# Two routings of a mixture-of-experts kernel: gate fills and ScalarE's order in the first, the layout of the list and the place of small steps in the second

## The chip, the core and the metric

The kernel runs on one core of one Trainium2 chip. A core has five engines, each with its own queue of instructions that it works through in order: TensorE (PE in the profile, its weight loads PEld), VectorE (DVE), ScalarE (ACT), GpSimd (POOL) and SyncE (SP), which here only starts DMAs. The metric is device time in microseconds (us). The kernel before takes 647.91 us, the median of three runs of 646.74 to 649.23.

## The reference

```python
X = np.fft.fft(x, axis=1); X = np.fft.fft(X, axis=2)      # x: 8 x 3072 x 256
x = X.real.reshape(24576, 256)
# first mixture: 8 experts, 256 -> 1024 -> 256
P = exp(x @ w_gate - max)
for _ in range(8):                                         # rows, then columns
    P /= P.sum(1) + 1e-9;  P /= P.sum(0) + 1e-9;  P *= N / E
x = sum over e of P[:, e] * (relu(x @ w1[e]) @ w2[e])
# second mixture: each row to the one expert with the largest logit
e = argmax(x @ w_gate2);  g = softmax(x @ w_gate2)[e]
out[row] = g * (relu(x[row] @ u1[e]) @ u2[e])
```

The logits are so spread that nearly all weights of the first mixture are zero in float32. The kernel computes the few (row, expert) pairs that count, and checks that there are not more than it has room for; otherwise a dense version would run.

## The kernel before, in words

There are five stages. The Fourier stage (lines 23 to 279) makes the transformed rows, writes them to the DRAM tensor H and keeps the 194 x 8 logits of each partition in SBUF. The first routing (`route1`) finds the pairs that count, gives each a slot in one of 29 tiles of 128 rows (three per expert and five free ones), and writes the row number of each slot into the list `Rhidx`. GpSimd then gathers the rows from H, and the first experts run. The second routing (`route2`) assigns the 29 tiles' rows to the second experts and makes the list `Rgidx` of 30 tiles; the rows are gathered from the DRAM tensor acc, and the second experts run, which scatter to the output. Each expert is a first product (line 914, eight blocks of 1024 hidden columns), relu into a high and a low part (lines 900 on ScalarE and 901 through the helper line 438 on VectorE), and a second product (line 947), with each float32 operand split into two parts.

A list is made by matmuls. VectorE makes for each slot column a 0/1 table `ah` of the row within a tile (`irx` compared with `rb`, 24, 24 and 16 columns at a time in the first routing, 10, 10 and 9 in the second) and a 0/1 table `oh` of the tile (`itx` compared with `tb`). From `oh` come two values, both in the tile `bv`: one by VectorE (times the entry `ja` or `t1`), one by ScalarE (times the partition number). TensorE multiplies `ah` of a column with both values of it, one matmul for each column, all added up in one PSUM tile `pl` (line 569 in the first routing, where values lie in runs of four columns, line 562 in the second, where a tile's columns lie 29 apart). VectorE reads the sums and writes the list.

While VectorE works on the first routing, TensorE has filler work: sixteen gate fills (`gates2`, line 1277), each 8 float32 matmuls that prepare the second gate's columns `g2` from the tables `w2t` of the eight experts, two fills for each, evicted from PSUM by ScalarE (line 1279) into two PSUM buffers in turn. The tables of experts 0 to 2 and 6 lie in the buffers rawa, rawb, rawc, and rawc again; those of 3, 4, 5 and 7 in `w1h`/`w1l` and `w2h`/`w2l`. The second fill of an expert below 4 issues the next load on SP's queue. The string table `G2` says where the fills stand: entry k is issued by `fill(k)` at the k-th hook of `route1` ("g" is a fill, "0" to "3" a piece of the first expert's weights whose high part ScalarE makes and whose low part is kept for VectorE later, "l" writes the logits to DRAM, "z" zeroes parts of the output and of acc, "v" is two warm-up matmuls with zeros).

At the end of a routing the rows of the first expert's three tiles come by gathers of 128 rows each (line 816), are turned by six transposes (line 867, `moe.turn`), and taken from PSUM by ScalarE as `xh` (line 870) and VectorE as `xl`; then line 914 begins. Warm-up matmuls (line 1296, `warm(n)`: n matmuls of 512 columns with zeros) stand before and after the list of the second routing (W3 and W4 of them) and between the transposes (three after each pair). `Slots` hooks small steps between the blocks of an expert: slot (0, i) comes after block i of the first product of expert 0.

Of the kernel before, what the change touches and what calls it, by code (L numbers as in the profile page):

```python
# [9 lines left out]
BF16 = mybir.dt.bfloat16  # L10
I32 = mybir.dt.int32
AF = mybir.ActivationFunctionType
ALU = mybir.AluOpType
# [350 lines left out]
NSL = 40  # L364
NS2 = 8
NSA = NSL + 3 * NS2
# [80 lines left out]
class Route:  # L447
# [5 lines left out]
    def C(self, n):  # L453
        a, w = self.K["off"][n]
        return self.K["cst"][:, a:a + w]

    def positions(self, T, M, n, rst, nf_, hook=lambda: None, S=None, n1=None):

# [15 lines left out]
        if two:  # L474
# [14 lines left out]
        nc.vector.tensor_tensor_scan(pos.rearrange("p e s -> p (e s)"), rst, m2.rearrange("p e s -> p (e s)"),  # L489
                                     0.0, ALU.mult, ALU.add)  # L490
        o.ts(oi, oi, 7, ALU.logical_shift_right)
# [38 lines left out]

    def split(self, T, gp, cs, n, nm):

        o = self.o
        a, g = T([n], name="ga" + nm), T([n], name="gs" + nm)
        tb, rb = T([n], BF16, name="tb" + nm), T([n], BF16, name="rb" + nm)
# [9 lines left out]
        return tb, rb, gp  # L545

# [25 lines left out]
def route1(nc, rt, L, rmx, K, R, keep, pool, ring, hooks):  # L572
# [88 lines left out]
    def spans(g0, g1, by):  # L661
        g = slice(g0, g1)
        wide = lambda v: v.rearrange("p (g s) -> p g s", s=RUN)[:, g, None, :].to_broadcast([128, g1 - g0, NT1, RUN])
        o.tt(oh[:, g], K["itx"][:, g], wide(tb), ALU.is_equal)
        o.tt(bv[:, g, 0], oh[:, g], wide(ja), ALU.mult)
        nc.scalar.activation(out=bv[:, g, 1], in_=oh[:, g], func=AF.Copy, scale=C(by))

    pl = rt.pt.tile([128, 512], F32, name="pt")
    a = late = None
    for n in CH1:  # L670
        if a is None:
            a = NSL
            spans(GL, GA, "p128")
        else:
            if a == NSA:
                spans(0, GL, "p")
            a %= NSA
        ah = rt.rows(ring, rb, a, n)
        if late is None:
            hooks[3]()  # L680
        late = late or ah
        rt.runs(pl, ah, bv, a, n, a == NSL, a + n == NSL)
        a += n
        if a == NSA:
            hooks[5]()
    hooks[4]()
# [68 lines left out]
def route2(nc, rt, lg, K, R, pool, ring, arrive, more, counts, warm):  # L755
# [5 lines left out]
    w8 = T([8], name="w8")  # L761
    t1 = T([NT1], BF16, name="t1")
    o.ts(w8, C("i8"), -1.0, ALU.mult, 8.0, ALU.add)
    o.cp(t1, C("at"))
# [26 lines left out]
    gp, later = rt.positions(T, M, NT1, C("rst2"), NF2, during)  # L791
    tb, rb, _ = rt.split(T, gp, (cs, ca), NT1, "b")
# [378 lines left out]
def run(tc, ctx, A, out, H, acc, Ld, Pd, Gd, Zd):  # L1171
# [62 lines left out]
    with tc.manual_schedule():  # L1234
# [27 lines left out]
        with ExitStack() as st:  # L1262
# [50 lines left out]
            with ExitStack() as s1:  # L1313
# [41 lines left out]
                fill(0)()  # L1355
                def low(k):
                    for f in lows[k]:
                        f()
                    lows[k].clear()
# [40 lines left out]
            with ExitStack() as s1:  # L1400
                moe.xp = P(st, "xp2", 2, side="right")
                r2 = P(s1, "r2", 1)
                ring = lambda n: xg.tile([128, CAP, HW], F32, name="Xg").rearrange("p a b -> p (a b)").bitcast(BF16)[:, :n]
                K["itx"] = r2.tile([128, NT2, NT1], BF16, name="itx2")
                K["irx"] = r2.tile([128, 128, max(CH2)], BF16, name="irx2")
                nc.scalar.activation(out=K["itx"], in_=rt.C("it")[:, :NT2, None].to_broadcast([128, NT2, NT1]), func=AF.Copy)
                nc.scalar.activation(out=K["irx"], in_=rt.C("i128")[:, :, None].to_broadcast([128, 128, max(CH2)]), func=AF.Copy)
# [48 lines left out]
            with ExitStack() as s1:  # L1456
                moe.fp = P(s1, "fp2", 1)
                yb = P(s1, "yb2", 4)
                moe2(nc, R, out, moe, W, part, X, xg, *rows("u1", "u2"), yb, check, grab2, xt)
    flag = nc.values_load(fi[0:1, 0:1], min_val=0, max_val=1)  # L1460
# [148 lines left out]
def moe1(nc, K, R, rt, lg, hot, acc, moe, W, part, X, xg, Gd, w1f, w2f, xb, pt, zeros, zt, rest, ask, trash, warm, grow):  # L1609
# [188 lines left out]

def moe2(nc, R, out, moe, W, part, X, xg, w1f, w2f, yb, check, grab, xt):
    o = Ops(nc)  # L1800
# [90 lines left out]
```

## Time and profile before

| | us |
|---|---|
| median of three runs (lowest, highest) | 647.91 (646.74, 649.23) |
| the profiled execution's own time | 648.06 |
| its span in the trace | 646.3 |

The span by stages, cut by hand where the stage's first matmul starts; engines' busy time and TensorE's granted clock (1.00 is 2.4 GHz, 0.50 is 1.2 GHz):

| stretch, us | length | PE | DVE | ACT | POOL | clock |
|---|---|---|---|---|---|---|
| 0 to 197.6, Fourier | 197.60 | 194.46 | 130.79 | 98.39 | 27.53 | 0.98 |
| 197.6 to 247.4, first routing | 49.80 | 44.44 | 36.57 | 15.39 | 10.13 | 0.86 |
| 247.4 to 430.1, first experts | 182.70 | 176.96 | 147.76 | 111.31 | 62.32 | 0.99 |
| 430.1 to 458.4, second routing | 28.30 | 26.22 | 14.07 | 7.01 | 10.64 | 0.95 |
| 458.4 to 646.3, second experts | 187.90 | 180.46 | 106.47 | 96.54 | 87.29 | 0.99 |

TensorE's busy time in the two routings is fillers and warm-up matmuls for the greater part, so it says little there; which engine is waited for is read from the waits in the timeline. The profile's chain of waits holds only the last scatter and its queue (shares of 0%), so it says nothing of the routings.

### The profile page before, as it was taken

The page shows a single profiled execution, that of the slowest core. Times are in us where ns is not written, and L with a number is a line of the kernel's source. Part 1 is how long each engine was busy: PE and PEld are TensorE (multiplying, and loading weights), DVE is VectorE, ACT ScalarE, POOL GpSimd, SP SyncE. Part 2 cuts the span into 40 slices and gives each one's busy share as a digit, 9 for nine tenths or more (in the row PEclk, how much of TensorE's full clock was granted, in tenths as well). Part 3 has the DMA queues.
Part 4 walks back from the last instruction along what each step waited for, and adds up shares of the span by engine and source line. Part 5 has one row for each costly group of instructions (what it writes and reads, how often), then busy time and mean ns, then how long its engine had stood idle before and what let it go on. Part 6 is the DMA issues. An engine that isn't in the chain of part 4 may idle for free. (4 is left out here: it accounts for less than half of the span.)

```text
span 646.3 us, 12642 instructions
## 1 busy us (share of the span) xinstructions
PE 622.5 (96%) x4790; PEld 600.1 (93%) x4790; DVE 435.7 (67%) x979; ACT 328.6 (51%) x756; POOL 197.9 (31%) x318
## 2 busy tenths in 40 slices
PE   9999999999999998999999999999899999999995
PEld 6889999999999898899899999987799999999995
DVE  3696877788247956768898796857455754854760
ACT  3344555555544413457575568642355654654651
POOL 0002201221011038882201011323687655312422
PEclk9998999999999778999999999999899999999999
DMA  8999999989989966598868888862565458347421
GB/s 207 274 244 288 266 279 285 272 260 291 344 311 285 413 203 222 148 327 273 278 240 321 306 305 232 205 185 43 168 229 196 159 205 302 141 170 277 153 101 38
DMA packets 56928, 152.57 MB, mean 236 GB/s; under 512 B 8308, under 2 KB 25852, under 8 KB 49437
## 3 DMA queue, kind: packets, MB, share of 16 engines
q1 hardware_dynamic: 47644, 114.69, 57.3%
q0 software_dynamic: 8752, 36.50, 16.7%
q8 instruction: 40, 0.66, 0.4%
q10 hardware_dynamic: 464, 0.51, 0.2%
q14 instruction: 28, 0.22, 0.1%
HBM read 101.50 MB, written 50.07 MB: 235 GB/s over the span
## 5 line engine op out<-in xcount | busy, mean ns | idle before, releaser
L438 DVE SCALAR_TENSOR_TENSOR hl<-ph,hh 128x384 fp32r<-128x384 f32 (+1 forms) x161 | 85.0, 544 | 77.8 <-ACT hh L900 65.3
L947 PE MATMUL py<-w2h,hh 128*128 128x256 f32 (+1 forms) x472 | 136.0, 288 | 0.9 <-ACT lg L1674 0.9
L947 PE MATMUL py<-w2h,hl 128*128 128x256 f32 (+1 forms) x472 | 133.6, 283 | 1.3 <-DVE hl L438 1.3
L947 PE MATMUL py<-w2l,hh 128*128 128x256 f32 (+1 forms) x472 | 133.1, 282 | 0.3 <-DVE w2l L852 0.3
L900 ACT ACTIVATE hh<-ph 128x384 fp32r<-128x384 f32 (+1 forms) x161 | 76.0, 481 | 57.7 <-PE ph L914 29.8
L947 PEld LDWEIGHTS py<-w2h,hl 128*128 128x128 f32 x472 | 88.8, 188 | 2.1 <-DVE hl L438 1.9
L947 PEld LDWEIGHTS py<-w2h,hh 128*128 128x128 f32 x472 | 89.0, 188 | 1.5 <-ACT lg L1674 1.4
L947 PEld LDWEIGHTS py<-w2l,hh 128*128 128x128 f32 x472 | 89.0, 189 | 0.5 <-DVE w2l L852 0.5
L914 PE MATMUL ph<-xh,w1h 128*128 128x384 f32 x256 | 68.2, 348 | 4.0 <-DVE hl L438 2.6
L914 PE MATMUL ph<-xh,w1l 128*128 128x384 f32 x256 | 65.7, 338 | 0.0
L914 PE MATMUL ph<-xl,w1h 128*128 128x384 f32 x256 | 65.6, 338 | 0.0
L74 PE MATMUL pp<-ca,w 96*128 96x96 f32 x512 | 61.2, 281 | 0.5 <-ACT at L76 0.5
L74 PEld LDWEIGHTS pp<-ca,w 96*128 96x128 f32 x512 | 60.2, 197 | 1.2 <-issue 0.7
L126 POOL TENSOR_TENSOR lc<-hd 128x32 f32<-128x32 f32 x23 | 9.0, 393 | 165.9 <-ACT hd L122 151.8
L821 POOL DMA_INDIRECT out_dram<-y,Rorow x30 | 33.1, 1104 | 85.2 <-ACT hh L900 47.1
L914 PEld LDWEIGHTS ph<-xh,w1h 128*128 128x128 f32 x256 | 45.5, 191 | 6.8 <-DVE hl L438 4.2
L84 DVE COPY t<-pp 128x512 f32<-128x512 f32 (+2 forms) x56 | 33.3, 608 | 23.3 <-PE pp L82 23.3
L91 PE MATMUL pp<-cb,t 128*128 128x128 f32 x368 | 47.5, 276 | 0.6 <-DVE t L84 0.6
L76 ACT ACTIVATE at<-pp 128x384 f32<-128x384 f32 x64 | 31.0, 491 | 33.4 <-PE pp L74 32.8
L914 PEld LDWEIGHTS ph<-xh,w1l 128*128 128x128 f32 x256 | 46.9, 190 | 0.0
L914 PEld LDWEIGHTS ph<-xl,w1h 128*128 128x128 f32 x256 | 46.5, 189 | 0.0
L816 POOL DMA_INDIRECT Xg<-H,Rhidx x29 | 32.2, 1109 | 43.8 <-DVE sb L433 38.3
(346 smaller groups left out, 1281.3 us busy)
## 6 DMA issues: line engine op xcount, KB each, us to landing
out_dram<-zt SPq DMA_DIRECT2D x48, 512.0 KB
H<-hd SPq DMA_DIRECT2D x24, 562.0 KB
xa<-in_xa_dram SPq DMA_DIRECT2D x32, 384.0 KB
xm<-in_xm_dram SPq DMA_DIRECT2D x32, 384.0 KB
rawa<-in_w_dram SPq DMA_DIRECT2D x8, 1024.0 KB
rawb<-in_w_dram SPq DMA_DIRECT2D x8, 1024.0 KB
rawa<-in_u_dram SPq DMA_DIRECT2D x8, 1024.0 KB
rawb<-in_u_dram SPq DMA_DIRECT2D x8, 1024.0 KB
```

The source lines that it names most:

```text
L74: nc.tensor.matmul(p[:M, i], lhs(4 * h + i), ca, start=True, stop=True)
L76: nc.scalar.activation(out=at[:M, :, :, s0:s0 + 4], in_=p[:M].rearrange("m s g j -> m g j s"), func=AF.Copy)
L84: nc.vector.tensor_copy(out=t[:, :n, :M], in_=p[:, :n, :M])
L91: nc.tensor.matmul(p[:M, i * 128:(i + 1) * 128], t[:, i, :M], cb[:, (g0 + i) * 128:(g0 + i + 1) * 128], start=True, stop=True)
L126: eng.tensor_tensor(out=lc[:np_, :n], in0=hd[:np_, :, 129:137], in1=hd[:np_, :, 273:281], op=ALU.add)
L438: self.nc.vector.scalar_tensor_tensor(out, a, s, b, op0, op1)
L816: nc.gpsimd.indirect_dma_start(out=out, out_offset=None, in_=src, in_offset=bass.IndirectOffsetOnAxis(ap=idx, axis=0))
L821: nc.gpsimd.indirect_dma_start(out=dst, out_offset=bass.IndirectOffsetOnAxis(ap=idx, axis=0), in_=src, in_offset=None, **kw)
L900: self.nc.scalar.activation(out=a[:, :n], in_=p[:, :n], func=AF.Relu)
L914: self.nc.tensor.matmul(p[:, :N], w, xx, start=(i == 0), stop=(i == 5))
L947: self.nc.tensor.matmul(p[:, :nd], c, W[2 + m // 4][w][:, m % 4, :nd], start=(m == 0 and i == 0), stop=(m == 7 and i == 2))
```

## The change

In the first routing the fills are dealt out anew (`G2`): seven in place of six stand before the counts' matmuls (line 470); three in the next entry, now between the weight pieces; two before the list's matmuls (the four warm-up matmuls "vv" are gone); none between the list's first 24 and its other 40 matmuls; two after the list, and the last one after the 24 small matmuls of `signs` (line 569 on `bq`). Both halves of `bv` are issued on ScalarE before the two fills' evictions. The load of expert 7's table, issued with the second fill of expert 3, now comes ahead of "l" and "z" in SP's queue.

On ScalarE in the first routing (g_76 is an eviction of a fill, bv the list's second value in its two halves, w2h a high part, xh the turned rows), before:

```order
L844 ACTIVATE w2h<-rawb 128x4x256
L847 ACTIVATE w2h<-g_76 128x4x8
L1279 ACTIVATE g_76<-py 128x32 x2
L666 ACTIVATE bv<-oh,cst 128x6x116
L1279 ACTIVATE g_76<-py 128x32 x3
L666 ACTIVATE bv<-oh,cst 128x10x116
L1279 ACTIVATE g_76<-py 128x32 x3
L870 ACTIVATE xh<-pt 128x384 x2
```

and now:

```order
L846 ACTIVATE w2h<-rawb 128x4x256
L849 ACTIVATE w2h<-g_76 128x4x8
L669 ACTIVATE bv<-oh,cst 128x6x116
L669 ACTIVATE bv<-oh,cst 128x10x116
L1281 ACTIVATE g_76<-py 128x32 x5
L872 ACTIVATE xh<-pt 128x384 x2
```

The second half of bv stood behind three evictions; it now follows the first half, and the five evictions that are left follow it.

In the first experts, the two low parts of the second weight of expert 0 (`rest[3](1)`, each two operations on VectorE) were both issued at slot (0, 0); now one is at slot (0, 0) and one at (0, 2).

In the second routing, three changes are on VectorE. The constants cs and ca, four operations ahead of the counts, become a precomputed `top` and three operations between the small ones that follow the scan; a memset of the padding is added. On VectorE around the counts (m a copy of the marks M, oi and pos made from it and from the counts' matmul in pt, ovc, inb and exb small steps behind the scan, cs and ca the constants), before:

```order
L441 COPY m_5477<-M 128x232
L435 TENSOR_SCALAR cs<-km 128x29
L429 TENSOR_TENSOR cs<-cs,Rprim 128x29
L433 TENSOR_SCALAR cs<-cs 128x29
L435 TENSOR_SCALAR ca<-cs 128x29
L435 TENSOR_SCALAR oi<-pt 128x8
L429 TENSOR_TENSOR m_5477<-m_5477,pt 128x8
L489 SCALAR_TENSOR_TENSOR pos<-cst,m_5477 128x232
```

and now:

```order
L441 COPY m_5476<-M 128x232
L435 TENSOR_SCALAR oi<-pt 128x8
L429 TENSOR_TENSOR m_5476<-m_5476,pt 128x8
L489 SCALAR_TENSOR_TENSOR pos<-cst,m_5476 128x232
L433 TENSOR_SCALAR oi<-oi 128x8
L429 TENSOR_TENSOR pos<-pos,M 128x232
L441 CAST ovc<-oi 128x8
L438 SCALAR_TENSOR_TENSOR cs<-km,Rprim 128x29
L494 SCALAR_TENSOR_TENSOR inb<-cst,ovc 128x8
L429 TENSOR_TENSOR cs<-cs,top 128x29
L429 TENSOR_TENSOR exb<-inb,ovc 128x8
L435 TENSOR_SCALAR ca<-cs 128x29
```

The four operations left the place between the copy and oi; three stand between ovc, inb and exb.

The tables oh and bv are laid out in runs of four columns as in the first routing, padded from 29 to 32 columns (960 in place of 870 elements), so that the list's matmuls read their values four elements apart. And the low part of the first piece of u2 (w2l) goes from behind the list to slot (0, 0) of the second experts. On VectorE behind the list (Rgidx the list, xl and hl low parts of the rows and of the hidden blocks), before:

```order
L429 TENSOR_TENSOR Rgidx<-pt,d 128x30
L850 TENSOR_TENSOR w2l<-rawb,w2h 128x4x256
L429 TENSOR_TENSOR xl<-pt,xh 128x384 x2
L433 TENSOR_SCALAR nf<-inb 128x1
...
L441 CAST Rfrow<-wr 128x6
L438 SCALAR_TENSOR_TENSOR hl<-ph,hh 128x384 x2
L850 TENSOR_TENSOR w2l<-rawb,w2h 128x4x256
```

and now:

```order
L429 TENSOR_TENSOR Rgidx<-pt,d 128x30
L429 TENSOR_TENSOR xl<-pt,xh 128x384 x2
L433 TENSOR_SCALAR nf<-inb 128x1
...
L441 CAST Rfrow<-wr 128x6
L438 SCALAR_TENSOR_TENSOR hl<-ph,hh 128x384
L852 TENSOR_TENSOR w2l<-rawb,w2h 128x4x256
L438 SCALAR_TENSOR_TENSOR hl<-ph,hh 128x384
L852 TENSOR_TENSOR w2l<-rawb,w2h 128x4x256
```

The first w2l went from ahead of xl to between the first two hl.

On TensorE there the warm-up matmuls are 14 ahead of the list (16 before) and 16 behind it (14 before), and the three behind the last pair of transposes are gone.

The diff, cut to its core:

```diff
-    def positions(self, T, M, n, rst, nf_, hook=lambda: None, S=None, n1=None):
+    def positions(self, T, M, n, rst, nf_, hook=lambda: None, S=None, n1=None, between=()):
...
-        o.cp(ovc, oi)
-        nc.vector.tensor_tensor_scan(inb, self.C("one8"), ovc, 0.0, ALU.mult, ALU.add)
-        o.tt(exb, inb, ovc, ALU.subtract)
-        o.stt(dab, exb, 128.0, self.C("dab"), ALU.mult, ALU.add)
+        for f in (lambda: o.cp(ovc, oi), lambda: nc.vector.tensor_tensor_scan(inb, self.C("one8"), ovc, 0.0, ALU.mult, ALU.add),
+                  lambda: o.tt(exb, inb, ovc, ALU.subtract), lambda: o.stt(dab, exb, 128.0, self.C("dab"), ALU.mult, ALU.add)):
+            f()
+            if between:
+                between.pop(0)()
...
     (route1)
-    a = late = None
+    a, late = NSL, None
+    spans(NSL // RUN, GA, "p128")
     for n in CH1:
-        if a is None:
-            a = NSL
-            spans(GL, GA, "p128")
-        else:
-            if a == NSA:
-                spans(0, GL, "p")
-            a %= NSA
         ah = rt.rows(ring, rb, a, n)
         if late is None:
+            late = ah
+            spans(0, GL, "p")
             hooks[3]()
-        late = late or ah
         rt.runs(pl, ah, bv, a, n, a == NSL, a + n == NSL)
-        a += n
-        if a == NSA:
-            hooks[5]()
+        a = (a + n) % NSA
...
     (route2)
+    top = T([NT1], name="top")
+    o.ts(top, R["prim"], 8 * 128.0 * CAP, ALU.mult, -1.0, ALU.add)
...
+    at = (lambda: o.stt(cs, km, -128.0 * CAP, R["prim"], ALU.mult, ALU.mult), lambda: o.tt(cs, cs, top, ALU.add),
+          lambda: o.ts(ca, cs, 1.0 / 128, ALU.mult, -127.0 / 256, ALU.add))
     def during():
-        o.ts(cs, km, -128.0 * CAP, ALU.mult, 8 * 128.0 * CAP, ALU.add)
-        o.tt(cs, cs, R["prim"], ALU.mult)
-        o.ts(cs, cs, -1.0, ALU.add)
-        o.ts(ca, cs, 1.0 / 128, ALU.mult, -127.0 / 256, ALU.add)
         more(counts[3])
         warm()
+    tp = T([NP], BF16, name="tp")
+    V.memset(tp[:, NT1:], -1.0)
...
-    oh = rt.tiles(T, tb, NT1)
-    bv = T([2, NT2, NT1], BF16, name="bv2")
-    o.tt(bv[:, 0], oh, t1[:, None, :].to_broadcast([128, NT2, NT1]), ALU.mult)
-    nc.scalar.activation(out=bv[:, 1], in_=oh, func=AF.Copy, scale=C("p"))
+    oh, bv = T([G2N, NT2, RUN], BF16, name="oh"), T([G2N, 2, NT2, RUN], BF16, name="bv2")
+    wide = lambda v: v.rearrange("p (g s) -> p g s", s=RUN)[:, :, None, :].to_broadcast([128, G2N, NT2, RUN])
+    o.tt(oh, K["itx"], wide(tb), ALU.is_equal)
+    o.tt(bv[:, :, 0], oh, wide(t1), ALU.mult)
+    nc.scalar.activation(out=bv[:, :, 1], in_=oh, func=AF.Copy, scale=C("p"))
...
-        rt.put(pl, ah, bv, a, n, a == 0, a + n == NT1)
+        rt.runs(pl, ah, bv, a, n, a == 0, a + n == NT1)
...
     (run)
-                signs, later = route1(nc, rt, L, rmx, K, R, S, r1, ring, [fill(i) for i in range(1, 5)] + [lambda: lows[0].pop(0)(), fill(6)])
+                signs, later = route1(nc, rt, L, rmx, K, R, S, r1, ring, [fill(i) for i in range(1, 5)] + [lambda: low(0, 1)])
...
                 fill(5)()
+                signs()
+                fill(6)()
                 assert not half
-                signs()
...
-                part("u", 0, 2, nc.vector)
-                xt = moe.turn(lambda i: X[0][:, i], lambda i: warm(3))
+                behind = []
+                part("u", 0, 2, nc.vector, behind)
+                xt = moe.turn(lambda i: X[0][:, i], lambda i: warm(3) if i < CAP - 1 else None)
...
-G2 = ("g", "", "gggggg", "0lz12g3gg", "ggvv", "ggg", "g")
+G2 = ("g", "", "ggggggg", "0lg1zg2g3", "gg", "gg", "g")
-W2, W3, W4 = 0, 16, 14
+W2, W3, W4 = 0, 14, 16
...
     (moe1)
-    for i, f in zip((0, 1, 3, 4), (lambda: rest[3](1), rest[0], rest[1], begin)):
+    for i, f in zip((0, 1, 2, 3, 4), (lambda: rest[3](1, 1), rest[0], lambda: rest[3](1), rest[1], begin)):
...
     (moe2)
+    sl.at(0, 0, *behind)
     sl.at(0, 1, lambda: part("u", 0, 3, V))
```

## Rows read from the trace of the kernel before

**Rows 1.** Windows: stretch, length, busy time of five engines, TensorE clock, DMA share, GB/s.

```profile
213.00:219.80 6.80, 6.76 (x36) 6.76 (x36) 6.49 (x20) 4.33 (x7) 0.00 (x0) 0.50 1.00 414
233.50:240.30 6.80, 6.80 (x39) 6.80 (x38) 5.81 (x36) 0.20 (x1) 4.10 (x4) 0.50 0.26 75
455.40:458.70 3.30, 3.30 (x11) 1.88 (x11) 0.62 (x2) 0.87 (x2) 2.39 (x3) 0.50 0.44 118
247.40:430.10 182.70, 176.96 (x1260) 171.41 (x1261) 147.76 (x373) 111.31 (x280) 62.32 (x87) 0.99 0.80 260
```

**Rows 2.** Timeline, TensorE, first routing: start, length, line, tiles, count, [wait before it and releaser].

```profile
202.33 3.74 PE L1277 MATMUL py<-wg,rawb 128*128 128x96 f32 x32
...
212.78 0.17 PE L470 MATMUL pt<-cd,trib 128*128 128x8 bf16 x1 [1.35 <-DVE cd L444]
...
226.18 1.79 PE L569 MATMUL pt<-bv,ah 128*128 128x58 bf16 x24
...
231.24 2.80 PE L569 MATMUL pt<-bv,ah 128*128 128x58 bf16 x40 [1.43 <-ACT bv L666]
233.86 3.71 PE L1277 MATMUL py<-wg,rawc 128*128 128x96 f32 x16
...
244.37 0.42 PE L867 MATMUL pt<-ident,x 128*128 128x128 f32 x2
...
247.43 1.07 PE L914 MATMUL ph<-xh,w1h 128*128 128x384 f32 x2 [1.37 <-ACT xh L870]
```

**Rows 3.** Timeline, ScalarE, first routing.

```profile
214.73 2.00 ACT L844 ACTIVATE w1h<-rawa 128x1024 fp32r<-128x1024 f32 x2 [2.11 <-DMA rawa<-in_w_dram]
217.29 1.06 ACT L844 ACTIVATE w2h<-rawb 128x1024 fp32r<-128x1024 f32 x1 [0.56 <-DMA rawb<-in_w_dram]
...
229.84 0.20 ACT L1279 ACTIVATE g<-py 128x32 f32<-128x32 f32 x1 [4.13 <-PE py L1277]
229.94 1.25 ACT L666 ACTIVATE bv<-oh,cst 128x1160 bf16<-128x1160 bf16 x1
```

**Rows 4.** Timeline, VectorE, first routing.

```profile
223.76 2.89 DVE L429 TENSOR_TENSOR ah<-irx,rba 128x3072 bf16<-128x3072 bf16 x2
...
234.08 0.19 DVE L435 TENSOR_SCALAR j<-pt 128x29 int32<-128x29 f32 x1 [6.30 <-PE pt L569]
...
239.10 0.18 DVE L429 TENSOR_TENSOR bq<-oh,rbq 128x64 bf16<-128x64 bf16 x1
...
242.12 0.49 DVE L1618 TENSOR_TENSOR x<-Xg 128x127 f32<-128x127 f32 x2
```

**Rows 5.** Timeline, VectorE, second routing.

```profile
438.92 0.17 DVE L435 TENSOR_SCALAR cs<-km 128x29 f32<-128x29 f32 x1
...
444.98 2.29 DVE L429 TENSOR_TENSOR Xg<-irx,rbb 128x1280 bf16<-128x1280 bf16 x3
...
449.90 0.19 DVE L429 TENSOR_TENSOR Rgidx<-pt,d 128x30 int32<-128x30 f32 x1
450.01 1.22 DVE L850 TENSOR_TENSOR w2l<-rawb,w2h 128x1024 fp32r<-128x1024 f32 x1
```

**Rows 6.** Timeline, TensorE, second routing.

```profile
442.65 3.63 PE L1296 MATMUL py<-zb 128*128 128x512 bf16 x16
446.11 3.30 PE L562 MATMUL pt<-bv,Xg 128*128 128x60 bf16 x29
...
454.08 0.42 PE L867 MATMUL pt<-ident,Xg 128*128 128x128 f32 x2 [1.64 <-DMA Xg<-acc,Rgidx]
...
457.10 0.64 PE L867 MATMUL pt<-ident,Xg 128*128 128x128 f32 x2
...
458.45 0.84 PE L914 MATMUL ph<-xh,w1h 128*128 128x384 f32 x2
```

**Rows 7.** Timeline, GpSimd, second routing: the first two gathers of the second experts' rows.

```profile
450.36 1.75 POOL L816 DMA_INDIRECT Xg<-acc,Rgidx  x1 [7.68 <-DVE Rgidx L429]
452.42 0.98 POOL L816 DMA_INDIRECT Xg<-acc,Rgidx  x1 [0.30 <-issue]
```

More of the change, by code (lines that the diff above doesn't have):

```diff
@@ L490, in positions @@
                                      0.0, ALU.mult, ALU.add)
+        between = list(between)
         o.ts(oi, oi, 7, ALU.logical_shift_right)
         o.tt(pos, pos, M, ALU.mult)
-        o.cp(ovc, oi)
-        nc.vector.tensor_tensor_scan(inb, self.C("one8"), ovc, 0.0, ALU.mult, ALU.add)
-        o.tt(exb, inb, ovc, ALU.subtract)
-        o.stt(dab, exb, 128.0, self.C("dab"), ALU.mult, ALU.add)
+        for f in (lambda: o.cp(ovc, oi), lambda: nc.vector.tensor_tensor_scan(inb, self.C("one8"), ovc, 0.0, ALU.mult, ALU.add),
[3 more added lines that the diff above has]
+                between.pop(0)()
         o.stt(w, pos, 128.0 * CAP + 0.5, dab[:, :, None].to_broadcast([128, 8, n]), ALU.is_ge, ALU.mult)
@@ L529, in positions, with split @@
         return gp, later
[L531 removed]
+    def split(self, T, gp, cs, n, nm, tb=None):
         o = self.o
         a, g = T([n], name="ga" + nm), T([n], name="gs" + nm)
[L535 removed]
+        whole = tb
+        tb, rb = T([n], BF16, name="tb" + nm) if tb is None else tb[:, :n], T([n], BF16, name="rb" + nm)
         big = 1.5 * 2.0 ** 23
@@ L761, in route2 @@
     w8 = T([8], name="w8")
-    t1 = T([NT1], BF16, name="t1")
+    NP = -(-NT1 // RUN) * RUN
+    t1 = T([NP], BF16, name="t1")
     o.ts(w8, C("i8"), -1.0, ALU.mult, 8.0, ALU.add)
-    o.cp(t1, C("at"))
+    V.memset(t1, 0.0)
+    o.cp(t1[:, :NT1], C("at"))
     big, M = T([NT1], name="big"), T([8, NT1], name="M")
     o.ts(big, R["prim"], -16.0, ALU.mult, 16.0, ALU.add)
+    top = T([NT1], name="top")
+    o.ts(top, R["prim"], 8 * 128.0 * CAP, ALU.mult, -1.0, ALU.add)
     def choose(a, b):
@@ L780, in route2 @@
     cs, ca = T([NT1], name="cs"), T([NT1], name="ca")
+    at = (lambda: o.stt(cs, km, -128.0 * CAP, R["prim"], ALU.mult, ALU.mult), lambda: o.tt(cs, cs, top, ALU.add),
+          lambda: o.ts(ca, cs, 1.0 / 128, ALU.mult, -127.0 / 256, ALU.add))
     def during():
-        o.ts(cs, km, -128.0 * CAP, ALU.mult, 8 * 128.0 * CAP, ALU.add)
-        o.tt(cs, cs, R["prim"], ALU.mult)
-        o.ts(cs, cs, -1.0, ALU.add)
-        o.ts(ca, cs, 1.0 / 128, ALU.mult, -127.0 / 256, ALU.add)
         more(counts[3])
         warm()
+    tp = T([NP], BF16, name="tp")
+    V.memset(tp[:, NT1:], -1.0)
     more(counts[2])
-    gp, later = rt.positions(T, M, NT1, C("rst2"), NF2, during)
-    tb, rb, _ = rt.split(T, gp, (cs, ca), NT1, "b")
-    oh = rt.tiles(T, tb, NT1)
-    bv = T([2, NT2, NT1], BF16, name="bv2")
-    o.tt(bv[:, 0], oh, t1[:, None, :].to_broadcast([128, NT2, NT1]), ALU.mult)
-    nc.scalar.activation(out=bv[:, 1], in_=oh, func=AF.Copy, scale=C("p"))
+    gp, later = rt.positions(T, M, NT1, C("rst2"), NF2, during, between=at)
+    tb, rb, _ = rt.split(T, gp, (cs, ca), NT1, "b", tp)
+    G2N = -(-NT1 // RUN)
+    oh, bv = T([G2N, NT2, RUN], BF16, name="oh"), T([G2N, 2, NT2, RUN], BF16, name="bv2")
[3 more added lines that the diff above has]
+    nc.scalar.activation(out=bv[:, :, 1], in_=oh, func=AF.Copy, scale=C("p"))
     pl = rt.pt.tile([128, 512], F32, name="pt")
@@ L1355, in run, with low @@
                 fill(0)()
-                def low(k):
-                    for f in lows[k]:
-                        f()
-                    lows[k].clear()
-                signs, later = route1(nc, rt, L, rmx, K, R, S, r1, ring, [fill(i) for i in range(1, 5)] + [lambda: lows[0].pop(0)(), fill(6)])
+                def low(k, n=None):
+                    for f in lows[k][:n]:
+                        f()
+                    del lows[k][:n]
+                signs, later = route1(nc, rt, L, rmx, K, R, S, r1, ring, [fill(i) for i in range(1, 5)] + [lambda: low(0, 1)])
                 X = {}
@@ L1403, in run @@
                 ring = lambda n: xg.tile([128, CAP, HW], F32, name="Xg").rearrange("p a b -> p (a b)").bitcast(BF16)[:, :n]
-                K["itx"] = r2.tile([128, NT2, NT1], BF16, name="itx2")
+                K["itx"] = r2.tile([128, -(-NT1 // RUN), NT2, RUN], BF16, name="itx2")
                 K["irx"] = r2.tile([128, 128, max(CH2)], BF16, name="irx2")
-                nc.scalar.activation(out=K["itx"], in_=rt.C("it")[:, :NT2, None].to_broadcast([128, NT2, NT1]), func=AF.Copy)
+                nc.scalar.activation(out=K["itx"], in_=rt.C("it")[:, None, :NT2, None].to_broadcast([128, -(-NT1 // RUN), NT2, RUN]), func=AF.Copy)
                 nc.scalar.activation(out=K["irx"], in_=rt.C("i128")[:, :, None].to_broadcast([128, 128, max(CH2)]), func=AF.Copy)
@@ L1458, in run @@
                 yb = P(s1, "yb2", 4)
-                moe2(nc, R, out, moe, W, part, X, xg, *rows("u1", "u2"), yb, check, grab2, xt)
+                moe2(nc, R, out, moe, W, part, X, xg, *rows("u1", "u2"), yb, check, grab2, xt, behind)
     flag = nc.values_load(fi[0:1, 0:1], min_val=0, max_val=1)
@@ L1796, in moe1, with moe2 @@
     return q, more
-def moe2(nc, R, out, moe, W, part, X, xg, w1f, w2f, yb, check, grab, xt):
+def moe2(nc, R, out, moe, W, part, X, xg, w1f, w2f, yb, check, grab, xt, behind):
     o = Ops(nc)
```

2 lines of the change are left out of this document (1 added, 1 removed).

## The prediction, made before the changed kernel was run

> **What bounds the kernel now.** I read the stages first, then TensorE's timeline in the two routings, then that of the engine each wait names. The expert stages are TensorE's: in the first it is busy 176.96 of 182.70 us at a mean clock of 0.99 [rows 1], so what a routing gives back before it should come out at the end. In the first routing the reader is to see three things. TensorE waits 1.35 us for VectorE's counts at 212.78 and 1.43 us for ScalarE at 231.24 [rows 2], and soon after each wait its clock is at 0.50, which is 1.2 GHz, for 6.8 us [rows 1]; a fill, about 1.8 us at 2.4 GHz (3.74 for two), then takes 3.7 [rows 2]. The wait at 231.24 is for the second half of bv, which ScalarE begins at 229.94, straight behind an eviction that itself had waited 4.13 us for TensorE's next fill [rows 3]; VectorE had finished what that half needs before 223.76, and its last row tables at 226.65 (223.76 and 2.89), and then waits 6.30 us until the list's matmuls end [rows 4]. So the list is late by ScalarE's order. In the second routing TensorE is busy with warm-up until the list's matmuls and waits for the first gather at 454.08 [rows 6].
>
> **First routing, part by part.** *Seven fills ahead of the counts.* The wait began at 211.43. One more fill of 1.8 ends at 213.2, so the counts come at most 0.45 later; part of that matmul group waits for VectorE's second result anyway. I take 0.2 (0 to 0.45). The wait is gone, and with it, I take it, the half clock from 213.0 to 219.8.
>
> *Five fills up to the list.* At 2.4 GHz they run from about 213.5 to 222.5, where five took until 229.8 before. Their tables must be there: two loads of equal size landed at 214.73 and 217.29 [rows 3], so the third, for expert 6, lands near 219.85; the fill that reads it begins near 220.7. Expert 7's load now comes next in the queue, another 2.6 us, and is read after the list.
>
> *The list.* The first 24 matmuls (1.79 us, 0.075 each [rows 2]) run from 222.5 to 224.3. ScalarE begins the second half of bv at 223.8 at the latest and ends it by 225.1. VectorE's next 24 columns of row tables, 60% of 2.89, are done at 225.5: TensorE waits 1.2. Then 24 and 16 matmuls at 0.075 and 0.07 [rows 2], the last 16 from 227.3 on (their tables are done at 226.65): 228.4, and 228.6 with the 0.2. VectorE's j, at 234.08 before [rows 4], comes 5.5 earlier. What covered the waiting before, fill and warm-up, is not needed by the list; what is late next is VectorE's row tables.
>
> *From the list to the experts.* VectorE's steps behind j are the same, so its last bq ends at 239.28 - 5.5 = 233.8 and its last row tile at 242.61 - 5.5 = 237.1 [rows 4]. The gathers now meet the last zero writes in the DMA queues (their share was 0.26 of the time from 233.5 on [rows 1]); a microsecond there is hidden behind VectorE's steps up to bq. TensorE has two fills, 24 small matmuls (1.8) behind bq, one fill, and the transposes. At 2.4 GHz: fills to 232.2, small ones to 235.0, last fill to 236.8, transposes at 237.1, 7.3 before the 244.37 of now [rows 2]. But the new wait of 1.2 us ending at 225.5 is nearly as long as the two that a drop followed, 0.2 and 2.3 us after their ends. With one such drop, from about 226.7 to 233.5, the two fills end at 234.7, the small matmuls at 236.5, the last fill at 238.3: 6.1 earlier. I take 6.1. The lower end is all three fills at 1.2 GHz: 235.8, 237.6, 241.2, so 3.2. The upper is 7.3, and 1.7 more if the 3.06 us from the first transposes to the first expert matmul (244.37 to 247.43 [rows 2]) shrink to the 1.35 from the last pair in the second routing (457.10 to 458.45 [rows 6]): 9.0.
>
> *The low parts set apart in the first expert* are the same VectorE work two slots later, all of it ahead of the same second product: 0, within 0.3 either way, less than the spread of the above.
>
> **Second routing, part by part.** *Constants.* Four operations of 0.17 [rows 5] leave VectorE's path ahead of the list, three come back between small ones that wait for each other, a memset and 10% wider tables add 0.05 each (0.6 ns an element, from 2.29 us for 3840 [rows 5]): -0.3, between -0.7 and +0.3. It is covered by TensorE's warm-up.
>
> *List in runs.* 29 matmuls take 3.30 us, 0.114 each [rows 6], where the first routing's, of 58 instead of 60 columns and in runs of four, take 0.075. The stride is the difference I see; I take 0.075, 2.2 in all (the other end is 3.30). Two warm-up matmuls fewer (3.63 for 16 [rows 6]) let them begin 0.45 earlier, at 445.66, so they end at 447.85 in place of 449.41. VectorE's third table, at 447.27 before, with 0.7 of matmuls behind it, would not be later once the constants' 0.3 is off. Gain 1.55, between 0.45 and 1.55.
>
> *The low part behind the list.* The first gather takes GpSimd 1.75 us and lies beside that 1.22 us operation, the second 0.98 beside nothing on VectorE [rows 5, 7]. I take 0.77 as the operation's doing. The Trainium skill says otherwise (SBUF — State Buffer, Who interferes with whom): a copy in a two-port mode locks GpSimd out of writing descriptors, but a tensor_tensor, which this is, was not seen to stall such a DMA. By that rule the gather keeps its 1.75; it is a rival below. The rows landed 1.97 after the first gather's end (454.08), so now at 451.75; the 16 warm-up matmuls end at 451.5. The third gather started at 452.42 + 0.98 + 0.30 = 453.70 and landed near 456.65, but TensorE, at 1.2 GHz in its warm-up [rows 1], took it at 457.10 [rows 6]. With 2.3 less it is there at 454.3: 2.8 earlier.
>
> *Behind that*, without the three warm-up matmuls the experts can begin up to 0.4 sooner; the low part, 1.22, now lies on VectorE between the first two hidden blocks, where it can hold up TensorE by 0 to 1.22. I set one against the other, net 0 (-0.8 to +0.4). And a drop of 3.3 us [rows 1] that was spent in warm-up would, if it falls on expert matmuls, cost 1.65; I take off 0.4. The second routing gives 2.4, between -0.4 and 3.2.
>
> **The sum.** 6.1 and 2.4 are 8.5. The profiled execution took 648.06 with a span of 646.3, so 639.55; the median of the runs is 0.15 lower, so 639.4.
>
> **Rivals.** *The clock takes half of it back.* For it: every wait of over 1.3 us in these rows had a drop behind it, and after the change three waits stand close together (1.2 before the second part of the list, some 1 for bq, the turn). Then the first routing gives 3.2 and the second 2.4 less 1.25: 4.35, 643.6. Against it: fewer and shorter waits than before.
>
> *The gather is as long as before*, by that rule of the Trainium skill (SBUF — State Buffer, Who interferes with whom) or because it is the first after a pause: the second routing loses 0.77, 640.2. Against it: 1.75 beside 0.98 with the same shape.
>
> *The first routing's gain does not last*, because the first experts go by their weight loads: the DMA engines are busy 0.80 of that stage [rows 1]. Then only the second routing's remains, 645.5. Against it: TensorE is idle only 5.7 of 182.7 us there.
>
> *Slower.* Seven warm-up matmuls go (four before the list, three behind the transposes). If TensorE from the wait at 224.3 on stays at 1.2 GHz into the first expert's products, each microsecond of half clock costs 0.5; it decides once such a stretch is longer by 17 us than the 6.8 it replaces, since 8.5 is then gone; with 30 us more it is 654.4. Against it: no stretch in the trace is longer than 6.8.
>
> **How the numbers follow.** Forecast 0.60, own range 637 to 642; clock rival 0.19; gather 0.10; gain that does not last 0.06; slower 0.05. The least that a measurement of this kernel tells from no change is about 0.5%, 3.2 us: faster is below 644.7. The forecast, the gather and most of the clock rival lie there: 0.85; the rest of the clock rival and the gain that does not last are the same, 0.10; slower 0.05. For 8 in 10 the range goes from 636.3 (the upper ends of both routings in part) to the clock rival's 643.9.
>
> **What would show it.** In the first routing: no wait before the counts and a clock of 1.00 from 213 to 220; the second half of bv on ScalarE near 224; j near 228.6; the transposes between 237 and 239. In the second: 29 list matmuls in 2.2 us, a first gather of about 1.0, expert matmuls 2 to 3 us sooner after the list's start than now. It would be wrong if j came after 231, if the fills behind the list all ran at 0.50, or if the list's matmuls kept 0.114 each.

## The result: 639.48 us, 1.2% faster

The changed kernel's median is 639.48 us (638.12 to 641.63, four runs); the kernel before has 648.21 beside it. The ratio is 0.9879, interval 0.985 to 0.9908: 7.8 us off (6.0 to 9.7). The profiled execution has a span of 637.2 us, 9.1 less than the one before. I count from the matmul of the total, which stands behind the first of the first routing's fills. This is it before, at 200.16:

```profile
200.16 0.38 PE L587 MATMUL pt<-m,tri 1*128 1x1 f32 x2 [0.37 <-DVE m L444]
```

TensorE in the first routing of the changed kernel, timeline (start, length, line, tiles, count, wait and releaser):

```profile
198.85 0.38 PE L590 MATMUL pt<-m,tri 1*128 1x1 f32 x2 [0.37 <-DVE m L444]
...
211.74 0.17 PE L470 MATMUL pt<-cd,trib 128*128 128x8 bf16 x1
...
221.14 1.84 PE L572 MATMUL pt<-bv,ah 128*128 128x58 bf16 x24
224.28 2.88 PE L572 MATMUL pt<-bv,ah 128*128 128x58 bf16 x40 [1.29 <-DVE ah L429]
226.98 3.71 PE L1279 MATMUL py<-wg,rawc 128*128 128x96 f32 x16
...
239.05 1.49 PE L869 MATMUL pt<-ident,x 128*128 128x128 f32 x6
240.91 1.07 PE L916 MATMUL ph<-xh,w1h 128*128 128x384 f32 x2 [0.37 <-ACT xh L872]
```

ScalarE there, and VectorE:

```profile
221.79 1.26 ACT L669 ACTIVATE bv<-oh,cst 128x1160 bf16<-128x1160 bf16 x1 [1.73 <-DVE oh L429]
...
239.30 0.20 ACT L1281 ACTIVATE g<-py 128x32 f32<-128x32 f32 x1 [4.96 <-PE py L1279]
240.36 0.87 ACT L872 ACTIVATE xh<-pt 128x384 fp32r<-128x384 f32 x2 [0.87 <-PE pt L869]
```

```profile
222.47 2.89 DVE L429 TENSOR_TENSOR ah<-irx,rba 128x3072 bf16<-128x3072 bf16 x2
...
227.19 0.19 DVE L435 TENSOR_SCALAR j<-pt 128x29 int32<-128x29 f32 x1 [0.70 <-PE pt L572]
```

Counts and fills have no wait now; the list waits for VectorE's tables (1.29), no longer for ScalarE; j comes 28.34 us after the total's matmul where [rows 4] give 33.92. Windows of the changed kernel (columns as in [rows 1]):

```profile
45.70:52.60 6.90, 6.41 (x55) 6.23 (x54) 6.26 (x9) 3.46 (x8) 1.67 (x3) 1.00 0.91 236
212.00:220.00 8.00, 8.00 (x75) 8.00 (x73) 7.60 (x22) 5.69 (x13) 0.00 (x0) 1.00 1.01 412
223.97:244.30 20.33, 19.66 (x128) 19.16 (x129) 13.11 (x56) 1.95 (x6) 13.48 (x21) 0.50 0.76 253
```

The clock stays up where [rows 1] had 0.50 from 213.0, but behind the list it is at 0.50 for 20.3 us, into the first products of the experts. The first line is chance: the Fourier stage is unaltered, the changed kernel's second profile has 0.50 there again (45.3 to 55.6), and before it had this:

```profile
45.70:52.60 6.90, 6.90 (x33) 6.90 (x33) 4.12 (x6) 2.46 (x6) 0.00 (x0) 0.51 1.03 254
```

Second routing: TensorE, GpSimd, and VectorE at the start of the second experts.

```profile
436.16 3.20 PE L1298 MATMUL py<-zb 128*128 128x512 bf16 x13
439.19 1.92 PE L572 MATMUL pt<-bv,Xg 128*128 128x60 bf16 x29
...
445.07 0.43 PE L869 MATMUL pt<-ident,Xg 128*128 128x128 f32 x2 [0.50 <-DMA Xg<-acc,Rgidx]
...
448.39 0.83 PE L916 MATMUL ph<-xh,w1h 128*128 128x384 f32 x2 [0.47 <-ACT xh L872]
...
455.87 0.62 PE L916 MATMUL ph<-xh,w1h 128*128 128x384 f32 x2 [0.75 <-DVE hl L438]
```

```profile
442.06 1.02 POOL L818 DMA_INDIRECT Xg<-acc,Rgidx  x1 [5.85 <-DVE Rgidx L429]
```

```profile
451.40 1.22 DVE L852 TENSOR_TENSOR w2l<-rawb,w2h 128x1024 fp32r<-128x1024 f32 x1
...
453.00 1.22 DVE L852 TENSOR_TENSOR w2l<-rawb,w2h 128x1024 fp32r<-128x1024 f32 x1
...
455.25 1.02 DVE L438 SCALAR_TENSOR_TENSOR hl<-ph,hh 128x384 fp32r<-128x384 f32 x2 [0.67 <-ACT hh L902]
```

Against [rows 6, 7] the list takes 1.92 in place of 3.30, the first gather 1.02 in place of 1.75, and from the first warm-up matmul to the first expert matmul it is 12.23 in place of 15.80. The moved low part makes TensorE wait 0.75.

Where the 9.1 comes from: ahead of the routing 1.31 (200.16 to 198.85, chance), first routing 5.21 (47.27 to 42.06 from the total's matmul to the first expert matmul), first experts 0.0 (195.22 and 195.25 from the first expert matmul to the second routing's warm-up), second routing 3.57, second experts -0.96 (187.85 and 188.81 from their first matmul to the end).

### The profile page after: what moved, and what is told of

Same layout as the page of the kernel before. It is cut to its first block, busy times and chain, and to the rows that moved or that the text cites. A ratio compares the mean times of both kernels' runs of the same rounds, so it can differ in the third digit from the quotient of the medians.

```text
span 637.2 us, 12627 instructions
## 1 busy us (share of the span) xinstructions
PE 615.2 (97%) x4778; PEld 593.4 (93%) x4783; DVE 435.4 (68%) x981; ACT 328.6 (52%) x756; POOL 194.1 (30%) x318
## 5 line engine op out<-in xcount | busy, mean ns | idle before, releaser
L823 POOL DMA_INDIRECT out_dram<-y,Rorow x30 | 34.8, 1159 | 86.4 <-ACT hh L902 43.7
L74 PE MATMUL pp<-ca,w 96*128 96x96 f32 x512 | 59.0, 275 | 0.0
L74 PEld LDWEIGHTS pp<-ca,w 96*128 96x128 f32 x512 | 58.2, 192 | 0.5 <-ACT Z L97 0.2
L91 PEld LDWEIGHTS pp<-cb,t 128*128 128x128 f32 x368 | 44.4, 192 | 0.9 <-DVE t L84 0.8
```

What stands on the lines that cost most here:

```text
L74: nc.tensor.matmul(p[:M, i], lhs(4 * h + i), ca, start=True, stop=True)
L91: nc.tensor.matmul(p[:M, i * 128:(i + 1) * 128], t[:, i, :M], cb[:, (g0 + i) * 128:(g0 + i + 1) * 128], start=True, stop=True)
L823: nc.gpsimd.indirect_dma_start(out=dst, out_offset=bass.IndirectOffsetOnAxis(ap=idx, axis=0), in_=src, in_offset=None, **kw)
```

## Experiments

My theory: the two parts add up, the first by the list's earlier end, cut short by the clock, the second by list and gather. The rivals were the clock and a gain that is lost later.

**1. Each part alone.** One kernel has only the first routing's edits (G2, the loop of `route1`, the low parts apart), the other only the second's.

> The change of the first routing alone (fills dealt out anew, both halves of bv ahead of the evictions, low parts apart in the first experts); the second routing as before. Theory (the two parts add up): from the first fill behind the total (200.46 in the profile of before, 199.16 in that of the changed kernel) to the first expert matmul 41.75 us as in the changed kernel, where before had 46.97, all of it kept to the end: 5.2 us off, 643.0 where before has 648.2 (641.5 to 644.5). Rival (the first experts or the second routing give it back, or the gain of 1.30 us ahead of the routing belongs to the change): 646.5 or more, or 641.5 or less with the FFT stage 1.3 shorter in most runs.

> The change of the second routing alone; the first routing as before. Theory: from the first warm-up matmul to the first expert matmul 12.2 us where before had 15.8 (list of 29 in 1.9, first gather 1.0), then 0.5 to 1.0 lost in the second experts to the low part on VectorE: 2.6 us off, 645.6 (644.6 to 646.6). Rival (the clock's fall behind the list moves into the experts): no gain, 648.

Measured: first part 0.992 (0.9893 to 0.9948), 5.2 us off, as expected (it ran at 645.74 where before had 650.56); second part 0.9982 (0.9961 to 1.0003), 1.2 off (-0.2 to 2.5), less than the 2.6 expected. Its routing is as short as expected (12.27 from warm-up to experts), but from the experts' first matmul to the end its profile takes 189.86, 2.0 more than before: 0.5 by the wait for hl, 0.9 by two longer waits for the overflow weights' gather (0.55 and 0.56; before one of 0.19); the rest stays open. Executions of the same first routing, in us after the total's matmul (starts of the rows, as above):

| profile | first routing | j | first transposes | first expert matmul |
|---|---|---|---|---|
| before | old | 33.92 | 44.21 | 47.27 |
| second part alone | old | 34.02 | 44.35 | 47.51 |
| changed | new | 28.34 | 40.20 | 42.06 |
| first part alone | new | 28.36 | 39.46 | 43.34 |
| low part behind | new | 28.29 | 37.97 | 43.23 |
| old layout | new | 28.30 | 37.97 | 43.28 |
| changed, again | new | 28.36 | 38.18 | 41.73 |

j is 5.6 earlier every time; the transposes 5.5 (4.1 to 6.3) against the mean of the two old ones, the experts 4.7 (4.0 to 5.7).

**2. Warm-up in the list's wait, and in all waits.**

```diff
         rt.runs(pl, ah, bv, a, n, a == NSL, a + n == NSL)
+        if a == NSL:
+            hooks[5]()
         a = (a + n) % NSA
...
-... [fill(i) for i in range(1, 5)] + [lambda: low(0, 1)])
+... [fill(i) for i in range(1, 5)] + [lambda: low(0, 1), lambda: warm(6)])
```

In all waits, besides:

```diff
                 fill(5)()
+                warm(8)
                 signs()
                 fill(6)()
...
-W2, W3, W4 = 0, 14, 16
+W2, W3, W4 = 5, 14, 16
```

> The changed kernel with six warm-up matmuls between the first 24 matmuls of the first routing's list and the other 40, where TensorE waits 1.29 us for VectorE's row tables. Theory (that wait lets the clock fall, and 20 us at 0.50 follow): the clock stays at 1.00 until 230 at least, the two fills behind the list take 1.8 each, the transposes come at 237.2 where they came at 239.05, and the first products of the first expert run at full clock: up to 3.5 us less, 636.0; where the longer waits for bq and for the rows let the clock fall later, 1 to 2 us less. Rival (the small matmuls of the list themselves, 58 columns each, let it fall, whatever lies between): 0.50 from about 224 as now, 639.5.

> As the one with warm-up in the list, and eight more warm-up matmuls ahead of the 24 small ones on bq and five ahead of the transposes, where waits open once the fills run at full clock. Theory (waits let the clock fall): no stretch of 0.50 between 200 and 250, transposes at 237.2 to 237.8, 3 to 3.5 us less than the changed kernel: 636.2. Rival (the small matmuls do): 0.50 behind the list all the same, and the warm-up matmuls at half the clock, 13 of 0.43 us, put the transposes 2 us or more later: 641.5 or more.

Measured: 0.9853 (0.9813 to 0.9893) and 0.9899 (0.9861 to 0.9937). Windows with warm-up in the list:

```profile
224.00:238.00 14.00, 12.42 (x136) 11.45 (x136) 12.26 (x48) 1.83 (x5) 5.10 (x6) 1.00 0.92 339
238.20:248.40 10.20, 7.26 (x27) 6.77 (x27) 4.88 (x13) 1.88 (x5) 9.12 (x16) 0.50 0.63 187
```

The clock holds through the list and the fills, so the list's small matmuls alone don't bring it down; it falls 3 us after the next wait (1.26 ahead of the matmuls on bq). But the expected gain did not come: the time is that of the changed kernel, since the experts start no sooner (41.87 after the total's matmul). ScalarE and TensorE there:

```profile
242.42 0.20 ACT L1283 ACTIVATE g<-py 128x32 f32<-128x32 f32 x1 [8.03 <-remote]
243.23 0.87 ACT L874 ACTIVATE xh<-pt 128x384 fp32r<-128x384 f32 x2 [0.62 <-remote]
```

```profile
239.35 1.49 PE L871 MATMUL pt<-ident,x 128*128 128x128 f32 x6
243.78 1.07 PE L918 MATMUL ph<-xh,w1h 128*128 128x384 f32 x2 [2.94 <-ACT xh L874]
```

The last fill ended at 239.56 and its eviction came at 242.42, 2.9 us later; the row names no engine ("remote"). The 3.06 us from transposes to experts in [rows 2] holds the same lateness. There the last fill ended at 242.50, and the row names a transpose, which the eviction doesn't read:

```profile
245.82 0.20 ACT L1279 ACTIVATE g<-py 128x32 f32<-128x32 f32 x1 [4.88 <-PE pt L867]
```

With warm-up in all waits the clock holds until 240.7, but the warm-up ahead of the transposes needs the PSUM buffer that this late eviction frees, and puts them at 42.28:

```profile
241.28 1.44 PE L1300 MATMUL py<-zb 128*128 128x512 bf16 x3 [2.94 <-ACT g L1283]
```

**3. Why ScalarE starts late.** To the kernel with warm-up in the list, one short instruction of no use is added on ScalarE ahead of the routing (an 8-column copy), or 24 (three behind each of eight evictions of fills). In the changed kernel, without that warm-up, the last eviction and the store behind it are put behind xh.

```diff
+                for _ in range(1):
+                    nc.scalar.activation(out=K["trib"][:, :8], in_=K["tri"][:, :8], func=AF.Copy)
```

> The kernel with six warm-up matmuls in the list, and one ScalarE instruction of no use (8 columns of a table copied) put in at about 197, so that every later ScalarE instruction stands one place further down in its program. In the kernel with the six warm-up matmuls, TensorE ended the last fill at 239.3, but ScalarE evicted it only at 242.42, waiting for nothing the profile shows; it is the same place of ScalarE's program that waits in the kernel before (245.82 for a fill that ended at 242.5) and in the first routing's change alone (244.57 for 241.0). Theory (ScalarE's next block of instructions begins at that place, is asked for when an earlier instruction at a fixed distance is done, and takes some 8 us): the late place moves to the eviction one earlier, which is due at 234.2, some 8 us after the one at 226.0; the last eviction follows its fill at once, xh comes 1 to 1.5 us behind the transposes and the first expert matmul at most 2.0 us behind them where it was 4.4: 39.5 to 40.5 us after the fill that starts behind the total, 41.9 before; 1.5 to 2.5 us less time. Rival (the gathers or the transfers of that moment hold ScalarE up, or its wait is on something at a fixed time): the last eviction stays 3 us behind its fill, the same time as with the six warm-up matmuls alone.

> The kernel with six warm-up matmuls in the list, with 24 short ScalarE instructions of no use (three behind each of the first eight evictions of fills, between 198 and 212), so that what follows stands 24 places further down in its program. Theory (ScalarE's program comes in blocks, and a block's begin lies at the last eviction): the lateness moves to another instruction, the last eviction follows its fill within 0.3 us, the first expert matmul comes 1.4 to 2 us behind the first transposes. Rival (the moment decides, with the gathers' transfers and GpSimd's writing under way, not the place in the program): the last eviction or xh is late by 2 us or more as in the kernels without it.

```diff
-                    nc.scalar.activation(out=g2[:, e, 4 * q:4 * q + 4],
...
+                    def evict(p=p, q=q):
...
+                    if (e, q) == (E - 1, 1):
+                        kept.append(evict)
+                    else:
+                        evict()
...
                 def low(k, n=None):
+                    while k == 1 and kept:
+                        kept.pop(0)()
```

> The changed kernel, with ScalarE's eviction of the very last fill (and the store of the gate values behind it) issued after the turned rows xh of the first expert. In runs with the changed first routing that eviction came 3.3 to 4.2 us after its fill had ended (the one ScalarE instruction one place down in its program did not change that as expected: still 1.7 us late), and xh, issued behind it, as late. Theory (the eviction itself waits, for TensorE's signal of that last fill or for the gate tile): xh comes 0.9 us behind the first transposes, the first expert matmul 1.4 to 1.9 us behind them. Rival (ScalarE has no instructions at that moment, whichever they are): xh still 3 us or more late, the first expert matmul 4 to 5 us behind the first transposes.

Measured: with one, the experts start at 39.79, the last eviction still 1.5 us behind its fill's end (237.56 to 239.09); 0.987 (0.9828 to 0.9911). With 24, at 38.93 and in time; with the eviction behind xh, at 38.61 and in time (636.93 and 637.72 in one run each, where before had 643.69). ScalarE with 24:

```profile
237.50 0.20 ACT L1283 ACTIVATE g<-py 128x32 f32<-128x32 f32 x1 [5.05 <-PE py L1281]
238.56 0.87 ACT L874 ACTIVATE xh<-pt 128x384 fp32r<-128x384 f32 x2 [0.87 <-PE pt L871]
```

Each of the two theories got one of its runs, so neither is shown. Nor does a start in time show that the edit brought it: the unaltered changed kernel had one too, in its first profile (239.30, above).

**4. The three edits together** (warm-up in the list, the eviction behind xh, `PROB` (0, 1, 1) to (0, 2, 1)), and the changed kernel again.

> The changed kernel with three edits that the runs so far point to: six warm-up matmuls between the first 24 and the other 40 matmuls of the first list, the last fill's eviction behind xh, and the softmax step of the second row group of the second experts one slot later (behind two hidden blocks in place of one), since ScalarE's hidden blocks stood behind it while VectorE was at the low part. Theory (each takes its own wait away): first expert matmul 38.5 to 39.5 us after the total's matmul (42.06 in the changed kernel's profile, 43.2 to 43.3 in three more executions of the same first routing), no wait of 0.74 us for hl at 7.5 us into the second experts: 3 to 5 us below the changed kernel. Rival (the clock's fall moves on into the first products and takes it back, and ScalarE's late start was chance): within 1.5 us of the changed kernel.

> The changed kernel itself, unaltered, on the chip of the other runs. Theory (the first routing's change is worth 4 to 5 us and the second's 2 to 3): 0.987 to 0.991 of the kernel before; its first expert matmul, where ScalarE's last eviction is late by 3 us or more, 43 us after the total's matmul, and where it is not, 42. Rival (the 1.30 us that the first profile showed ahead of the routing, and its short way from the transposes to the experts, were luck that carried the result): 0.992 or more.

Measured: 0.987 (0.983 to 0.991) and 0.9869 (0.9815 to 0.9922): the three edits gain nothing over the changed kernel, as the rival had it. ScalarE of the three edits:

```profile
233.94 0.20 ACT L1286 ACTIVATE g<-py 128x32 f32<-128x32 f32 x1 [1.76 <-PE py L1283]
242.93 0.87 ACT L874 ACTIVATE xh<-pt 128x384 fp32r<-128x384 f32 x2 [8.79 <-remote]
```

xh, now first in line, is late itself, 4.2 us behind the first transposes (238.77). So it isn't the eviction that waits. The wait for hl shrinks from 0.75 to 0.16, as expected. TensorE and ScalarE of the changed kernel, again:

```profile
240.29 1.15 PE L869 MATMUL pt<-ident,x 128*128 128x128 f32 x6
```

```profile
243.12 0.20 ACT L1281 ACTIVATE g<-py 128x32 f32<-128x32 f32 x1 [5.88 <-remote]
243.29 0.87 ACT L872 ACTIVATE xh<-pt 128x384 fp32r<-128x384 f32 x2
```

The same program that was in time in its first profile is 2.7 us late here (its last fill ended at 240.46). So the place in ScalarE's program does not decide it. What does hold ScalarE shows in the times of TensorE's semaphore updates, which the trace keeps and no row prints: in every profile the last eviction, or xh where it is issued first, starts 0.02 to 0.03 us behind such an update. With the three edits the last fill and the six transposes end between 238.97 and 240.25, but their seven updates all come between 242.73 and 242.94; with the 24 instructions each update comes within 0.02 us of its matmul's end. So ScalarE is not late: TensorE's signal is. In eleven of the fourteen profiles the last fill's update is 1.5 to 4.8 us behind the fill's recorded end (ends of matmuls are modelled); in three (the changed kernel's first, the 24 instructions, the eviction behind xh) it is not. The eleven also hold only 640 to 652 updates of that semaphore, the three 674 or 675. Why the signals come late, whether the matmuls themselves end later than the record has it, and whether either would happen if nothing was recorded, stays open.

**5. The second routing's parts.** The low part back behind the list:

```diff
-                part("u", 0, 2, nc.vector, behind)
+                part("u", 0, 2, nc.vector)
```

> The changed kernel with the low part of u2's first piece back behind the second routing's list, where the kernel before has it. Theory (that operation on VectorE stretches the gather beside it): first gather 1.75 us on GpSimd where the changed kernel has 1.02, first transposes 0.7 us later after the first warm-up matmul (9.6 where it has 8.91), and the wait of 0.75 us for hl in the second experts back to 0.24. Rival (the first gather after a pause is long, or its length went with something else of the change): 1.02 still, transposes at 8.9.

GpSimd and VectorE of that kernel:

```profile
447.27 1.75 POOL L818 DMA_INDIRECT Xg<-acc,Rgidx  x1 [5.51 <-DVE Rgidx L429]
449.33 0.98 POOL L818 DMA_INDIRECT Xg<-acc,Rgidx  x1 [0.30 <-issue]
```

```profile
446.92 1.22 DVE L852 TENSOR_TENSOR w2l<-rawb,w2h 128x1024 fp32r<-128x1024 f32 x1
```

As the theory had it: the gather beside the operation takes 1.75, without it 1.02 (1.75 in all four profiles with the operation there, 1.01 to 1.02 in the ten without), transposes at 9.71 in place of 8.91; the wait for hl is back to 0.23. The Trainium skill (SBUF — State Buffer, Who interferes with whom) has it that a tensor_tensor was not seen to stall such a DMA, though with both inputs in SBUF it contends with GpSimd's reads; this run shows 0.73 us, and the measurement decides. Which part of the gather is held up no run shows.

The old layout of oh and bv, with the rest of the change:

```diff
-    oh, bv = T([G2N, NT2, RUN], BF16, name="oh"), T([G2N, 2, NT2, RUN], BF16, name="bv2")
...
+    oh = rt.tiles(T, tb, NT1)
+    bv = T([2, NT2, NT1], BF16, name="bv2")
...
```

> The changed kernel with the second routing's tables oh and bv laid out as before (the values of one list matmul 29 elements apart, 870 elements). Theory (the stride makes the list's matmuls slow): 29 matmuls in 3.3 us again, 0.114 each, where the changed kernel has 1.92; the first transposes 1.4 us later after the first warm-up matmul (10.3 where it has 8.91). Rival (the list goes by VectorE's tables, and the shorter matmuls only wait for them): 0.3 us later at most.

```profile
443.39 3.31 PE L565 MATMUL pt<-bv,Xg 128*128 128x60 bf16 x29
```

The list is back at 3.31. The first transposes come at 11.28, 2.4 later and not 1.4, since here the clock fell behind the list and the warm-up matmuls took longer. The list's 1.4 is the layout's. The low part behind, the old layout and the kernel of experiment 6 ran once each (644.68, 644.82 and 644.32 us, where before had a median of 648.93), so their traces are read here and not their times.

**6. ScalarE's order alone**, in the kernel before.

```diff
-            if a == NSA:
-                spans(0, GL, "p")
...
         if late is None:
+            spans(0, GL, "p")
             hooks[3]()
```

> The kernel before with one thing of the change: the second half of bv issued ahead of the two fills' evictions on ScalarE; the fill between the 24 and the 40 matmuls stays. Theory (the list is late by ScalarE's order): the second half of bv begins when VectorE has its oh, 223.8 where it was 229.94; the 40 matmuls follow the fill at 229.8 with no wait of 1.43; j comes 1.4 us earlier (32.5 us after the matmul of the total, where before has 33.92), no more, since the fill and the warm-up still stand ahead. If the wait also caused the half clock behind the list, the two fills there take 1.8 us each in place of 3.7 and 2.5. Rival (VectorE's tables are late too): j less than 0.5 earlier.

VectorE and then TensorE:

```profile
222.89 2.89 DVE L429 TENSOR_TENSOR ah<-irx,rba 128x3072 bf16<-128x3072 bf16 x2
...
230.95 0.19 DVE L435 TENSOR_SCALAR j<-pt 128x29 int32<-128x29 f32 x1 [4.04 <-PE pt L569]
```

```profile
228.10 2.81 PE L569 MATMUL pt<-bv,ah 128*128 128x58 bf16 x40
```

The wait of 1.43 is gone; j is 31.64 after the total's matmul, 2.3 earlier: 1.6 between the list's two parts, as the theory has it (1.4), and 0.7 ahead of the list, where the clock happened to be at 0.50 for 3.4 us and not 6.8. The fills behind the list now ran at 2.4 GHz. One of them waited for expert 7's table, whose load this kernel still has behind the other writes in SP's queue:

```profile
234.29 0.46 PE L1276 MATMUL py<-wg,w1l 128*128 128x96 f32 x2 [0.75 <-DMA w1l<-in_w2t_dram]
```

So the order is worth about 1.6 of the 5.6; the rest is the fills' places and the clock, which no run here parts.

## Why the prediction was right, step by step

*List and counts* came out to 0.3 us: counts 0.27 later (0.2 forecast), the wait for tables 1.29 (1.2), j 28.34 after the total's matmul (28.4 from 228.6). *Behind the list* the sizes were off: one drop of 6.8 was forecast, 6.1 us of gain at the transposes; the profiled execution was at 0.50 for 20.3 us and gained 4.0 there, the five of the table 5.5 by the mean. That both fills and the last ran at 0.50 is what the prediction had named as a sign that it was wrong; in the four other executions they did not all. (Its five fills "until 229.8" before are six: five had ended by 225.5. No term hangs on that.) *The 3.06 from transposes to experts* I carried over as it stood. It is no fixed price: it was 1.86 in the changed kernel and up to 5.3 elsewhere, as TensorE's signals to ScalarE came in time or late. So 1.2 of the profile's 5.21 is that they came in time there, and the first routing is worth 4.7 to the experts by the table, not 6.1; the term was mis-sized by the longer drop and by what the trace before already showed, an eviction at 245.82 of a fill that had ended at 242.50.

*The second routing* was forecast at 2.4 and its profile has 3.57 less 0.96. The list gave 1.38 and its earlier begin 0.43; the gather 0.73 (0.77 forecast); the low part, set at nothing net, costs 0.5 by the wait for hl. The other 1.05 lies between the first transposes and the experts (4.37 before, 3.32 now), where before had 3.4 us at 0.50 from 455.3 on and the new order had none in the profile. The timed value of this part alone, 1.2 (-0.2 to 2.5), holds the forecast at its upper end.

The total met the forecast to 0.1 us, and that was partly luck: the first routing is 1.4 smaller, the second's profile larger, and 1.31 of the profile's 9.1 lies ahead of both. By the ratios the two alone make 6.4, and both together 7.8 and 8.5 in two sets of runs; the intervals cover each other, and the forecast 8.5. *Rivals*: the clock took back some, not half; the gather rival is refuted by experiment 5; that the gain does not last is refuted for the first routing (0.0 lost in the first experts); the slower one did not come, though its "no stretch is longer than 6.8" did not hold for the changed kernel (20.3).

## What to carry to other kernels

Ask of each stage which engine ends it, then look behind it: once TensorE's list was early, the start of the experts hung on ScalarE, and ScalarE on signals of TensorE that came late. A gap that the profile puts down to nobody, or to something that the instruction doesn't read, is a price of its own and may not be moved along with its neighbours; look for the semaphore's own update before blaming the engine that waits. Where a stretch depends on the clock, take several profiles before giving it a size: the same first routing put the same transposes at 37.97 to 40.20, and one kernel had late signals in one profile and none in the other.

## What the runs showed of the hardware

Matmuls of 60 columns whose moving values lie 29 elements apart took 0.114 us each, four apart 0.066 (3.31 and 1.92 for 29). After waits of only 1.25 to 1.43 us in the first routing the clock fell to 0.50, 0.2 to 3.3 us after their end or while they lasted, and filling one wait moved the fall to the next. That is no rule: waits of 1.30 and 1.62 us ahead of the second routing's transposes (low part behind, 451.08; order alone, 451.29) had no fall behind them, and the old layout's fall at 446.50 had no such wait ahead. An indirect gather took 1.75 us beside a tensor_tensor of VectorE and 1.02 without. TensorE's semaphore updates for the first routing's last fill came 1.5 to 4.8 us behind its recorded end in eleven profiles of fourteen, and at once in three; ScalarE began 0.02 to 0.03 us behind the update in all.
